# Rounding the weights on GpSimd, one row-sum step per head pair, and early activations rounded on ScalarE: a fused attention and feed-forward kernel on Trainium2

## The chip, the core and the metric

The kernel runs on one core of one Trainium2 chip. A core has five engines with instruction queues of their own: TensorE (PE in the profile; its weight loads are PEld), VectorE (DVE), ScalarE (ACT), GpSimd (POOL) and SyncE (SP), which here issues nearly all DMAs. Each engine runs its queue in order, so an instruction that waits holds everything behind it. The metric is the device time of one execution in microseconds; lower is better. Before the change three timed executions gave 724.78, 723.21 and 723.17 us, median 723.21.

## The reference

```python
# attention: q, k, v of (4, 8, 768, 64) in float32
scores = scale * np.matmul(q, k.transpose(0, 1, 3, 2))
keep = is_sink | in_window            # 4 sink keys, window of 128
scores = np.where(keep, scores, -1000000000.0)
a = np.exp(scores - np.max(scores, axis=-1, keepdims=True))
a = a / (np.sum(a, axis=-1, keepdims=True) + 1e-09)
attn_out = np.matmul(a, v)
# feed-forward on x of (3072, 512), w_in (512, 2048), w_out (2048, 512)
h = x @ w_in
g = h * np.clip(h + 3.0, 0.0, 6.0) / 6.0
out = g @ w_out
```

The two weight matrices arrive as 64-bit floats, which the kernel reads as pairs of 32-bit integers.

## The kernel before

The work is cut into 12 units of 256 tokens (4 batches, 3 token blocks each). A unit has 4 pairs of heads, so there are 48 pairs, numbered s = 0 to 47; the first 16 pairs belong to the first token block of each batch, whose queries see only two key tiles. Pairs 0 to 9 are `plain`: their score, transpose and value products run in full float32 passes. After the 4 pairs of a unit come its feed-forward steps, i = 0 to 7, each on 256 of the 2048 hidden columns: 24 matmuls into `hps` (`ffn1`, line 468), then the activation, then 12 matmuls into the output accumulators `o` (`ffn2`, line 490).

Every product outside the plain pairs is made from rounded pieces. A value x is split into a high part, x rounded to the format `fp32r` that TensorE takes at full rate, and a low part, x minus the high part. `hps` is therefore summed from wih*xh, wih*xl and wil*xh, and `o` from gh*woh, gh*wol and g*woh.

The weights come in 32 pieces of 128x512, in the order wih, wih, woh, woh per step i. `load_part` (line 135) brings a piece into one of four buffers `st` by a DMA on SP, takes its 64-bit words apart on ScalarE (lines 153 and 157) and puts a 32-bit float together on VectorE (lines 159 and 161), in one of three buffers `wt`. Then `copy_r` (line 163) rounds it to the high part, on ScalarE before the change (`WHI = "A"`), and VectorE makes the low part (line 164). A buffer `st` is free for the next DMA when line 161 has read it.

For a plain pair the chain is: scores on TensorE into a PSUM bank (`sp`, line 306); masking and row minimum on VectorE (line 313); exponential and row sum on ScalarE (line 335), one instruction for each of the two query tiles t of each head h; 1e-9 added and the reciprocal taken on VectorE (lines 337, 338); scaling of each block by its reciprocal (`norm`, line 319); transposes on TensorE into `pt` (line 361), copied out by ScalarE as `pf` (line 365); the product with the values, `av` (line 428); and its split into xh and xl for the feed-forward (lines 443, 444). The blocks of t = 0 have 128 columns, those of t = 1 have 256. `NORM0 = "DADA"` gives the engine for the four blocks of pairs 0 to 8: VectorE for the 128-column ones, ScalarE for the 256-column ones; pair 9 and all later pairs scale on ScalarE.

The activation of a feed-forward step is: `gf` on ScalarE (line 476), times the clip on VectorE (line 477), rounded to `gh` (line 478, on VectorE by `GHI = "DD"`), and the low part `g` on VectorE (line 479). `eng` (line 206) takes the letter after the first for the units 0 to 2 (n*NP < START = 9), and the first letter for all later ones.

The loop over s (line 572) interleaves by the string `ORDER`: scores and softmax of pair s-1, values and feed-forward of pair s-2, weight pieces (one per s from 1 to 4, then four per s), and `drain` calls, which emit a feed-forward step only when its weight pieces have been emitted. While pairs 0 to 3 are under way there is no feed-forward work, and `keep_busy` puts dummy matmuls (`idle`) between the scores. The framework then orders the instructions of each engine by its own estimate of when their inputs are ready, so that a change of an engine also changes the order on the others.

Of the kernel before, what the change touches and what calls it, by code (L numbers as in the profile page):

```python
# [14 lines left out]
ALU = mybir.AluOpType  # L15
# [3 lines left out]
P = 128  # L19
# [13 lines left out]
def copy_r(nc, eng, out, src, scale=1.0):  # L33
    if eng is nc.scalar:
        nc.scalar.mul(out=out, in_=src, mul=scale)  # L35
    elif eng is nc.gpsimd:
        nc.gpsimd.tensor_scalar(out=out, in0=src, scalar1=scale, scalar2=1.0, op0=ALU.mult, op1=ALU.mult)
    elif scale != 1.0:
        nc.vector.tensor_scalar(out=out, in0=src, scalar1=scale, scalar2=None, op0=ALU.mult)
    else:  # L40
        nc.vector.tensor_copy(out=out, in_=src)  # L41
# [3 lines left out]
def attn_ffn_kernel(ctx: ExitStack, tc: tile.TileContext, qx, kx, vx, vfx, vsx, n_sink, window, w_in, w_out, out):  # L45
    nc = tc.nc
# [80 lines left out]
    WOH = [const.tile([P, 2, DM], F32R, name=f"woh{i}") for i in range(NFP)]  # L127
    WOL = [const.tile([P, 2, DM], F32R, name=f"wol{i}") for i in range(NFP)]
    wide = mybir.dt.size(w_in.dtype) == 8
    WHI, WLO = "A", "D"  # L130

    def weng(which, at):
        return {"D": nc.vector, "P": nc.gpsimd, "A": nc.scalar}[which[at % len(which)]]
# [65 lines left out]

    SSE = "DD"  # L200
    START = 9
    GHI, GLO = "DD", "DD"
    XHI, XLO = "DDA", "DD"
    KHI, KLO, QHI, QLO = "AA", "DD", "AA", "DD"

# [80 lines left out]
    def cell(s, h, t, c0, c1):  # L286

        if plain(s):
            return st_[s][f"P{h}"][:, t * P + c0:t * P + c1]
        return st_[s]["P"][:, h, t * WP + c0:t * WP + c1]  # L290
# [23 lines left out]
                                       scalar=3.0e38, op0=ALU.add, op1=ALU.min,  # L314
                                       accum_out=d["nb"][:, i:i + 1])

    NORM0, NORM = "DADA", "AAAA"

    def norm(e, blk, c):
        if e == "A":  # L320
            nc.scalar.mul(out=blk, in_=blk, mul=c)  # L321
        elif e == "D":
            nc.vector.tensor_scalar(out=blk, in0=blk, scalar1=c, scalar2=None, op0=ALU.mult)
        else:
            nc.gpsimd.tensor_scalar(out=blk, in0=blk, scalar1=c, scalar2=1.0, op0=ALU.mult, op1=ALU.mult)

    def C_soft(s, h):
# [5 lines left out]
        for t in range(2):  # L333
            i, blk = 2 * h + t, cell(s, h, t, *live[t])
            d["exp"] = nc.scalar.activation(out=blk, in_=blk, func=AF.Exp, scale=-1.0,  # L335
                                            bias=nb[:, i:i + 1], accum_out=sm[:, i:i + 1])
        nc.vector.tensor_scalar(out=sm[:, hs], in0=sm[:, hs], scalar1=1e-9, scalar2=None, op0=ALU.add)
        nc.vector.reciprocal(out=rc[:, hs], in_=sm[:, hs])
        if u:
# [2 lines left out]
            prior = d["P"][:, h, 0:2 * WP].rearrange("p (t w) -> p t w", t=2)[:, :, 0:P]  # L342
            nc.gpsimd.tensor_tensor(out=both, in0=both, in1=prior, op=ALU.add)  # L343
            live = [(P, W2), (P, W2)]
        for t in range(2):
            i, blk = 2 * h + t, cell(s, h, t, *live[t])
            norm((NORM0 if s < START else NORM)[i], blk, rc[:, i:i + 1])
        if u and h == 1:

            ss = ssc.rearrange("p (t k h y) -> p t k h y", t=2, k=2, h=2)  # L350
# [423 lines left out]
```

## Time and profile before

| | |
|---|---|
| median of three timed executions | 723.21 us |
| the profiled execution | 726.12 us |
| its span, first to last instruction | 724.4 us |
| mean granted TensorE clock, share of full speed | 0.996 |
| TensorE busy | 707.9 us, 98% |
| TensorE weight loads busy | 637.9 us, 88% |
| VectorE busy | 494.3 us, 68% |
| ScalarE busy | 424.8 us, 59% |
| GpSimd busy | 169.1 us, 23% |

The shares are means over stages that differ. The last of the weight pieces is finished at some 123 us; until then VectorE and ScalarE do the weights beside the attention of the first pairs and the first feed-forward steps, and GpSimd has nothing to do. From 190.77 us on GpSimd merges and masks blocks of the later pairs. Matmuls overlap in the array, so the duration of one matmul is longer than the distance from one to the next.

### The profile page before, as it was taken

To read this page: it belongs to the slowest core of one execution; us is meant where nothing else is said; L and a number is where in the kernel's file an instruction comes from. 1 tells how busy PE (TensorE), PEld (TensorE's weight loads), DVE (VectorE), ACT (ScalarE), POOL (GpSimd) and SP (SyncE) were. 2 spreads that over 40 slices of the span, in tenths; PEclk is the share of its full clock that TensorE was granted. 3 is DMA by queue.
4 is the path that set the end of the run, shared out by engine and by line. 5 is a ranking of instruction groups with operands and counts; after the bars stand their busy time and mean duration, and the time that the engine had idled before them with its cause. 6 is when DMAs were issued, how large, how long until landed. Compare 5 with 4: busy or idle time off the path is not lost. (4 is left out here: it accounts for less than half of the span.)

```text
span 724.4 us, 14312 instructions
## 1 busy us (share of the span) xinstructions
PE 707.9 (98%) x4772; PEld 637.9 (88%) x4772; DVE 494.3 (68%) x1418; ACT 424.8 (59%) x1139; POOL 169.1 (23%) x336
## 2 busy tenths in 40 slices
PE   8998999999999999999999999999999999999996
PEld 7777787899999999999998999999989999998985
DVE  5798999666775776775866777777676686532231
ACT  6998997656656657566655665655665665311211
POOL 1000000000143243353343343243344253100000
PEclk9999999999999999999999999999999999999999
DMA  7666683544545546445544644644644632000000
GB/s 239 190 190 213 208 249 101 143 108 133 131 124 141 130 120 173 117 113 140 142 108 125 161 119 104 176 109 125 170 107 109 164 81 61 30 1 1 30 1 34
DMA packets 55602, 89.11 MB, mean 123 GB/s; under 512 B 8416, under 2 KB 38368, under 8 KB 55520
## 3 DMA queue, kind: packets, MB, share of 16 engines
q1 hardware_dynamic: 55376, 88.11, 44.7%
q8 instruction: 40, 0.66, 0.4%
q14 instruction: 42, 0.34, 0.2%
q10 hardware_dynamic: 144, 0.00, 0.0%
HBM read 42.47 MB, written 6.29 MB: 67 GB/s over the span
## 5 line engine op out<-in xcount | busy, mean ns | idle before, releaser
L468 PE MATMUL hps<-xh,wih 128*128 128x256 f32 x768 | 221.1, 288 | 4.1 <-ACT wih L35 2.8
L468 PE MATMUL hps<-xh,wil 128*128 128x256 f32 x768 | 217.4, 283 | 0.2 <-DVE wil L164 0.2
L468 PE MATMUL hps<-xl,wih 128*128 128x256 f32 x768 | 216.3, 282 | 0.1
L490 PE MATMUL o<-woh,gh 128*128 128x512 f32 x384 | 154.8, 403 | 2.3 <-DVE gh L41 2.2
L468 PEld LDWEIGHTS hps<-xh,wih 128*128 128x128 f32 x768 | 144.9, 189 | 9.0 <-ACT wih L35 5.6
L490 PE MATMUL o<-wol,gh 128*128 128x512 f32 x384 | 151.3, 394 | 0.0
L490 PE MATMUL o<-woh,g 128*128 128x512 f32 x384 | 151.1, 395 | 0.0
L468 PEld LDWEIGHTS hps<-xl,wih 128*128 128x128 f32 x768 | 145.1, 189 | 0.9 <-DVE xl L444 0.3
L468 PEld LDWEIGHTS hps<-xh,wil 128*128 128x128 f32 x768 | 144.7, 189 | 0.7 <-DVE wil L164 0.4
L335 ACT ACTIVATE Pt<-Pt,nb 128x272 f32<-128x272 f32 (+2 forms) x152 | 76.9, 506 | 77.2 <-DVE nb L313 76.4
L343 POOL TENSOR_TENSOR Pt<-Pt 128x256 f32<-128x256 f32 x64 | 47.4, 740 | 274.8 <-ACT Pt L335 274.8
L477 DVE SCALAR_TENSOR_TENSOR gf<-gf,hps 128x512 f32<-128x512 f32 x96 | 65.8, 685 | 64.2 <-ACT gf L476 61.6
L476 ACT ACTIVATE gf<-hps,three 128x512 f32<-128x512 f32 x96 | 65.5, 683 | 71.5 <-PE hps L468 70.8
L490 PEld LDWEIGHTS o<-woh,g 128*128 128x128 f32 x384 | 72.2, 188 | 16.4
L490 PEld LDWEIGHTS o<-woh,gh 128*128 128x128 f32 x384 | 72.4, 189 | 13.9 <-ACT xh L35 1.6
L321 ACT ACTIVATE Pt<-Pt,rc 128x144 f32<-128x144 f32 (+2 forms) x152 | 55.7, 414 | 44.9 <-POOL Pt L343 39.5
L490 PEld LDWEIGHTS o<-wol,gh 128*128 128x128 f32 x384 | 72.4, 189 | 10.6
L479 DVE TENSOR_TENSOR g<-gf,gh 128x512 fp32r<-128x512 f32 x96 | 69.3, 722 | 1.2 <-PE o L490 0.3
L379 POOL TENSOR_SCALAR_AFFINE_SELECT ph<-ph 128x256 fp32r<-128x256 f32 x64 | 32.4, 510 | 153.0 <-ACT ph L35 153.0
L311 PE MATMUL sp<-K,Q 128*128 128x272 f32 (+2 forms) x304 | 61.5, 286 | 1.5 <-DMA Q<-qt 1.4
L313 DVE CUSTOM_DVE_ANT_0 Pt<-sp,m_t 128x272 f32<-128x272 f32 x128 | 54.0, 432 | 11.1 <-PE sp L311 10.2
L311 PEld LDWEIGHTS sp<-K,Q 128*128 128x128 f32 x304 | 51.4, 188 | 8.9 <-DVE xl L452 0.8
(96 smaller groups left out, 1080.6 us busy)
## 6 DMA issues: line engine op xcount, KB each, us to landing
K<-kt SPq DMA_DIRECT2D x128, 200.0 KB, 3.5
Q<-qt SPq DMA_DIRECT2D x152, 64.0 KB, 2.5
st<-in_w_in_dram SPq DMA_DIRECT2D x16, 512.0 KB, 4.1
st<-in_w_out_dram SPq DMA_DIRECT2D x16, 512.0 KB, 5.1
kr<-in_kx_dram SPq DMA_DIRECT2D x32, 200.0 KB, 2.5
qr<-in_qx_dram SPq DMA_DIRECT2D x48, 128.0 KB, 2.2
out_dram<-ost SPq DMA_DIRECT2D x24, 256.0 KB, 2.4
vr<-in_vx_dram SPq DMA_DIRECT2D x32, 192.0 KB, 2.5
```

The lines of the kernel that those rows point to most:

```text
L311: nc.tensor.matmul(out=sp[:, 0:w], lhsT=Q[:, h, t * P:(t + 1) * P], rhs=K[:, h, part, k0c:k0c + w], start=(part == 0), stop=(part == 1))
L313: d["min"] = nc.vector.tensor_tensor_reduce(out=cell(s, h, t, 0, w), in0=sp[:, 0:w], in1=m[:, 0:w], scale=-SCALE, scalar=3.0e38, op0=ALU.a ...
L321: nc.scalar.mul(out=blk, in_=blk, mul=c)
L335: d["exp"] = nc.scalar.activation(out=blk, in_=blk, func=AF.Exp, scale=-1.0, bias=nb[:, i:i + 1], accum_out=sm[:, i:i + 1])
L343: nc.gpsimd.tensor_tensor(out=both, in0=both, in1=prior, op=ALU.add)
L379: nc.gpsimd.affine_select(out=prior[i], in_=own[i], pattern=[[0, 2], [-1, P]], base=0, channel_multiplier=1, compare_op=ALU.is_gt, fill=0.0)
L468: nc.tensor.matmul(out=hp[:, half, :], lhsT=l, rhs=r, start=(j == 0), stop=(j == n - 1))
L476: nc.scalar.activation(out=gf, in_=hp, func=AF.Relu, bias=three, scale=1.0)
L477: nc.vector.scalar_tensor_tensor(out=gf, in0=gf, scalar=6.0, in1=hp, op0=ALU.min, op1=ALU.mult)
L479: eng(GLO, state["n"] * NP).tensor_tensor(out=g, in0=gf, in1=gh.bitcast(F32), op=ALU.subtract)
L490: nc.tensor.matmul(out=acc, lhsT=l[:, f, ts_], rhs=r[i][:, f, :], start=(i == 0 and f == 0 and j == 0), stop=(i == NFP - 1 and f == 1 and ...
```

## The change

Five edits. `copy_r` on GpSimd becomes a `tensor_copy` instead of a two-operand scaling (no call used GpSimd before). `WHI` goes from ScalarE to GpSimd: all 32 weight pieces get their high part there. `NORM0` goes from `DADA` to `PAPA`: the 128-column blocks of pairs 0 to 8 are scaled by GpSimd (line 325). In a plain pair the softmax end runs once per pair: after the exponentials of head 0 `C_soft` returns, and after those of head 1 the additions and reciprocals of all four sums are one instruction each on 128x4, followed by the four scalings. `GHI` goes from `DD` to `DA`: `gh` of units 0 to 2 is rounded on ScalarE.

```diff
     elif eng is nc.gpsimd:
-        nc.gpsimd.tensor_scalar(out=out, in0=src, scalar1=scale, scalar2=1.0, op0=ALU.mult, op1=ALU.mult)
+        nc.gpsimd.tensor_copy(out=out, in_=src)
...
-    WHI, WLO = "A", "D"
+    WHI, WLO = "P", "D"
...
-    GHI, GLO = "DD", "DD"
+    GHI, GLO = "DA", "DD"
...
-    NORM0, NORM = "DADA", "AAAA"
+    NORM0, NORM = "PAPA", "AAAA"
...
+        heads = [h]
+        if plain(s):
+            if h == 0:
+                return
+            heads, hs = [0, 1], slice(0, 4)
...
-        for t in range(2):
-            i, blk = 2 * h + t, cell(s, h, t, *live[t])
-            norm((NORM0 if s < START else NORM)[i], blk, rc[:, i:i + 1])
+        for g in heads:
+            for t in range(2):
+                i, blk = 2 * g + t, cell(s, g, t, *live[t])
+                norm((NORM0 if s < START else NORM)[i], blk, rc[:, i:i + 1])
```

In the changed file the lines behind the edits stand five or six lower: 337 and 338 are 342 and 343, 361 is 367, 428 is 434, 476 is 482. On VectorE, at the end of the softmax of pair 0 (`sm` holds the row sums, `rc` their reciprocals, `Ph` one head's blocks, `st` a weight piece), the difference reads:

```order
-L337 TENSOR_SCALAR sm<-sm 128x2
-L338 RECIPROCAL rc<-sm 128x2
-L323 TENSOR_SCALAR Ph<-Ph,rc 128x128
-L337 TENSOR_SCALAR sm<-sm 128x2
-L338 RECIPROCAL rc<-sm 128x2
-L323 TENSOR_SCALAR Ph<-Ph,rc 128x128
+L342 TENSOR_SCALAR sm<-sm 128x4
+L343 RECIPROCAL rc<-sm 128x4
 L159 SCALAR_TENSOR_TENSOR st<-st 128x512
```

Six instructions of VectorE become two, behind the exponentials of both heads. On TensorE, from the transposes of pair 1 to the scores of pair 2 (`pt` the transposes, `av` the value products of pair 0, `sp` the scores of pair 2), the difference reads:

```order
-L361 MATMUL pt<-ident_r,Ph 128x128 x4
+L434 MATMUL av<-pf,VF 128x256
+L434 MATMUL av<-pf,VF 128x128
+L434 MATMUL av<-pf,VF 128x256
+L434 MATMUL av<-pf,VF 128x128
+L367 MATMUL pt<-ident_r,Ph 128x128 x6
 L306 MATMUL sp<-kr,qr 128x128
 L306 MATMUL sp<-kr,qr 128x256
-L361 MATMUL pt<-ident_r,Ph 128x128 x2
 L81 MATMUL idle<-rel 128x128 x4
```

The scores of pair 2 stood between the transposes of pair 1, ahead of the last two; now they stand behind all six. On GpSimd, from the last of the mask copies on, there stood before:

```order
L187 COPY m_t_99<-m_t_98 128x128
L116 TENSOR_SCALAR m_t_98<-col 128x16
L189 COPY m_t_99<-m_t_98 128x128
L188 COPY m_t_99<-m_t_98 128x16
L343 TENSOR_TENSOR Pt<-Pt 128x2x128 x2
```

where the last row belongs to a pair of the second token block (190.77 us). Now, in the same place (`wih_111` and `woh_127` are the high parts of step 0, `wih_112` of step 1):

```order
L188 COPY m_t_99<-m_t_98 128x16
L325 TENSOR_SCALAR Ph<-Ph,rc 128x128 x2
L37 CAST wih_111<-wt 128x512 x2
L325 TENSOR_SCALAR Ph<-Ph,rc 128x128 x2
L37 CAST woh_127<-wt 128x512
L325 TENSOR_SCALAR Ph<-Ph,rc 128x128 x2
L37 CAST woh_127<-wt 128x512
L37 CAST wih_112<-wt 128x512
L325 TENSOR_SCALAR Ph<-Ph,rc 128x128 x2
L37 CAST wih_112<-wt 128x512
```

A stretch of 32 casts and 18 scalings now stands ahead of the row of line 343 (348 in the changed file); both casts of step 0's wih stand ahead of the scalings of pair 1. The third place is the first activation of a feed-forward step (`hps` its matmuls' sum, `wol` the low part of a weight piece). On VectorE there stood before:

```order
L477 SCALAR_TENSOR_TENSOR gf<-gf,hps 128x512
L313 ISA Ph,nb<-sp,m_100 128x128
L313 ISA nb 128x1
L41 CAST gh<-gf 128x512
L164 TENSOR_TENSOR wol_136<-wt,woh_128 128x512
L479 TENSOR_TENSOR g<-gf,gh 128x512
```

The rounding `gh` is on ScalarE in the changed order, whose rows there read:

```order
L482 ACTIVATE gf<-hps,three 128x512
L35 ACTIVATE pf<-pt 128x384
L157 ACTIVATE st<-st 128x512
L153 ACTIVATE wt<-st 128x512
L35 ACTIVATE gh<-gf 128x512
```

Between `gf` and `gh` the queue of ScalarE holds a copy and two weight instructions of other work, and VectorE's part of `gf` lies in between; before, `gh` followed on the same engine.

## Rows read from the trace of the kernel before

**Rows 1.** Busy time by stretch (window in us, its length, then busy us and number of instructions of PE, PEld, DVE, ACT and POOL, mean granted TensorE clock, DMA share, GB/s): the first pairs, the first feed-forward steps, the rest of the weight stage, and 100 us from the middle.

```profile
0.00:34.00 34.00, 31.71 (x197) 25.97 (x198) 23.21 (x97) 25.91 (x74) 3.09 (x16) 1.00 0.67 216
34.00:80.00 46.00, 40.68 (x231) 32.48 (x229) 41.01 (x106) 40.60 (x95) 0.00 (x0) 0.96 0.63 195
80.00:132.40 52.40, 51.27 (x325) 44.05 (x324) 48.76 (x130) 46.54 (x116) 0.00 (x0) 1.00 0.62 183
...
300.00:400.00 100.00, 100.00 (x694) 91.56 (x693) 70.30 (x209) 61.11 (x173) 38.51 (x72) 1.00 0.52 130
```

**Rows 2.** What TensorE waited for from 0 to 133 us (instruction, what released it: us in total, times, longest).

```profile
PE hps L468 <- ACT wih L35: 2.8, 3, 2.2
PE o L490 <- DVE gh L41: 2.2, 2, 1.4
...
PE hps L468 <- DVE gf L477: 0.9, 1, 0.9
...
PE pt L361 <- ACT Ph L321: 0.3, 1, 0.3
```

**Rows 3.** TensorE alone around its longest wait (window, length, busy us, granted clock, DMA share, GB/s).

```profile
61.70:63.90 2.20, 0.01 (x1) 0.94 0.08 18
63.90:67.10 3.20, 3.18 (x13) 0.51 0.51 166
```

**Rows 4.** Instructions in order of time (start, duration, engine, line, what; in brackets the idle time before and what ended it) that lead to this wait: SP's queue, ScalarE and VectorE.

```profile
54.36 0.93 SPq L148 DMA_DIRECT2D st<-in_w_out_dram  x2
...
59.52 0.66 ACT L153 ACTIVATE wt<-st 128x512 f32<-128x512 f32 x1 [1.27 <-DMA st<-in_w_out_dram]
...
63.24 0.62 ACT L35 ACTIVATE wih<-wt 128x512 fp32r<-128x512 f32 x1
...
60.71 0.17 DVE L337 TENSOR_SCALAR sm<-sm 128x2 f32<-128x2 f32 x1 [1.37 <-ACT Ph L335]
...
61.90 0.68 DVE L161 SCALAR_TENSOR_TENSOR wt<-wt,st 128x512 int32<-128x512 int32 x1
```

**Rows 5.** Groups of instructions from 0 to 132.4 us (line, engine, operation, tiles, shapes, count, busy us, mean ns of one, idle before and releaser), on VectorE and, the last, on ScalarE.

```profile
L159 DVE SCALAR_TENSOR_TENSOR st<-st 128x512 int32<-128x512 int32 x32 | 21.9, 686 | 1.7 <-ACT st L157 1.7
L161 DVE SCALAR_TENSOR_TENSOR wt<-wt,st 128x512 int32<-128x512 int32 x32 | 21.4, 685 | 0.1
L164 DVE TENSOR_TENSOR wil<-wt,wih 128x512 fp32r<-128x512 f32 x16 | 10.9, 687 | 1.0 <-ACT wih L35 0.9
L164 DVE TENSOR_TENSOR wol<-wt,woh 128x512 fp32r<-128x512 f32 x16 | 10.9, 686 | 1.0 <-ACT woh L35 0.9
...
L323 DVE TENSOR_SCALAR Ph<-Ph,rc 128x128 f32<-128x128 f32 x18 | 5.1, 283 | 0.3
L41 DVE CAST gh<-gf 128x512 fp32r<-128x512 f32 x11 | 4.6, 421 | 0.2 <-PE o L490 0.2
...
L35 ACT ACTIVATE wih<-wt 128x512 fp32r<-128x512 f32 x16 | 10.0, 622 | 0.0
```

**Rows 6.** Pairs of rows in order of time from which the distance of one start to the next is read, where the engine had no pause: a weight rounding on ScalarE; the rounding `gh` on VectorE; and row sum, reciprocal and scaling of one head on VectorE, with the next instruction behind them.

```profile
38.85 0.63 ACT L35 ACTIVATE wih<-wt 128x512 fp32r<-128x512 f32 x1
39.36 0.69 ACT L476 ACTIVATE gf<-hps,three 128x512 f32<-128x512 f32 x1
...
42.73 0.42 DVE L41 CAST gh<-gf 128x512 fp32r<-128x512 f32 x1
43.07 0.68 DVE L164 TENSOR_TENSOR wol<-wt,woh 128x512 fp32r<-128x512 f32 x1
...
17.56 0.16 DVE L337 TENSOR_SCALAR sm<-sm 128x2 f32<-128x2 f32 x1
...
18.16 0.42 DVE L444 TENSOR_TENSOR xl<-av,xh 128x256 fp32r<-128x256 f32 x1
```

**Rows 7.** Pair 1 in order of time: TensorE's transposes, the scores of pair 2 and the last transposes; and on ScalarE the last exponential and the last scaling of pair 1.

```profile
18.30 0.33 PE L361 MATMUL pt<-ident_r,Ph 128*128 128x128 f32 x1 [0.58 <-DVE Ph L323]
18.56 0.92 PE L306 MATMUL sp<-kr,qr 64*128 64x128 f32 x4
19.41 0.44 PE L361 MATMUL pt<-ident_r,Ph 128*128 128x128 f32 x2
...
16.50 0.49 ACT L335 ACTIVATE Ph<-Ph,nb 128x256 f32<-128x256 f32 x1
...
18.35 0.50 ACT L321 ACTIVATE Ph<-Ph,rc 128x256 f32<-128x256 f32 x1
```

**Rows 8.** Groups on GpSimd over the whole span (columns as in rows 5): its only cast to `fp32r`, and its scaling instructions of 128 columns.

```profile
L116 POOL TENSOR_SCALAR m_t<-rel 128x128 bf16<-128x128 f32 x2 | 0.6, 298 | 4.5 <-DVE rel L112 4.5
...
L72 POOL CAST ident_r<-ident 128x128 fp32r<-128x128 f32 x1 | 0.3, 293 | 0.1
```

**Rows 9.** GpSimd and VectorE beside each other at 309 to 313 us, in order of time, and the group of VectorE's `qt` from 40 to 122 us, while GpSimd had no work.

```profile
309.59 0.40 POOL L379 TENSOR_SCALAR_AFFINE_SELECT pl<-pl 128x256 fp32r<-128x256 f32 x1
...
312.02 0.89 POOL L381 TENSOR_SCALAR_AFFINE_SELECT pl<-pl 128x256 fp32r<-128x256 f32 x1
...
309.62 0.65 DVE L30 TENSOR_TENSOR qt<-qr,qt 128x256 fp32r<-128x256 f32 x1
...
311.96 0.69 DVE L479 TENSOR_TENSOR g<-gf,gh 128x512 fp32r<-128x512 f32 x1
...
L30 DVE TENSOR_TENSOR qt<-qr,qt 128x256 fp32r<-128x256 f32 x2 | 0.8, 420 | 0.0
```

## The prediction

> **What bounds the kernel now.** I read the page's first two sections first, then the busy times by stretch, then what TensorE waited for, then the order of time around the waits. TensorE is busy 98% of the span, so nothing that only makes another engine shorter is worth anything, unless TensorE waits for it. The reader should look for the difference between the length of a stretch and TensorE's busy time in it [rows 1]: 34.00 - 31.71 = 2.3 us in the first stretch, 46.00 - 40.68 = 5.3 in the second, 52.40 - 51.27 = 1.1 in the third, and nothing from 300 to 400 us. The order of TensorE's instructions before and after the change is the same from the instruction that runs at 132.4 us on, and the instructions ahead of it are the same ones in another order, so the change can move only what TensorE loses in the first 132.4 us. There VectorE (41.0 of 46 us, then 48.8 of 52.4) and ScalarE (40.6, then 46.5) are as full as an engine in a queue of waits gets [rows 1], and they feed TensorE's weights and activations.
>
> The waits name it [rows 2]: 2.8 us for a rounded weight piece `wih`, 2.2 for `gh`, 0.9 for a buffer that `gf` frees, 0.3 and (the row at 18.30 [rows 7]) 0.58 for scaled blocks. The longest, 2.20 us at 61.7, also costs clock: in the 3.20 us behind it the granted clock was 0.51, the 1.2 GHz level [rows 3], so 3.18 us of matmuls took about 1.6 us longer than at full clock. What the change could win at most is therefore 0.9 (scaled blocks) + 5.3 + 1.1 + 1.6 = 8.9 us, 8.0 of them from 34 us on.
>
> **The change part by part.** The sum is made against the profiled execution, 726.12 us with a span of 724.4; the median of the runs shown is 723.21, 2.9 lower, and I subtract the same amount from it.
>
> Weights on GpSimd. ScalarE loses 32 roundings at one start per 0.51 us (38.85 to 39.36 [rows 6]), 16.3 us. GpSimd gets 32 casts of 512 columns. The trace has no such cast; the nearest rows are a cast of 128 columns at 0.293 us [rows 8] and a one-input select of 256 at 0.40 [rows 9]. That is 0.107 for 128 columns more, so 512 columns take about 0.40 + 2 x 0.107 = 0.61 us as an estimate; the same select beside VectorE took 0.89, which would make the cast 0.61 + 0.49 = 1.10. I take 0.61 to 1.10, and 0.8 as the middle, because VectorE is at work nearly all the time there. 32 x 0.8 = 26 us on an engine that is idle in this stage [rows 1]: this by itself costs nothing. On the path of a piece it replaces a wait in ScalarE's queue. At the long stall line 161 ended at 61.90 + 0.68 = 62.58, ScalarE began the rounding at 63.24 and ended at 63.86 [rows 4]; GpSimd would end it at about 63.4.
>
> Scalings on GpSimd and one softmax end per pair. For each head VectorE spent 0.60 us on sum, reciprocal and scaling (17.56 to 18.16 [rows 6]); 18 such heads in pairs 0 to 8 are 10.8 us, of which nine pairs keep two instructions of 0.2, so 7.2 us go, and 0.4 for pair 9: 7.6. GpSimd gets 18 scalings at 0.30 [rows 8], 5.4 us.
>
> `gh` on ScalarE. VectorE loses 0.34 us (42.73 to 43.07 [rows 6]) for each of 11 roundings up to 132.4 us [rows 5], 3.7 us; the other 13 come later, where ScalarE is 61% busy [rows 1] and has room. ScalarE gets 11 x 0.51 = 5.6 us. So in the weight stage ScalarE is relieved of 16.3 - 5.6 = 10.7 us and VectorE of 7.6 + 3.7 = 11.3.
>
> What GpSimd takes back from VectorE. Where both work at once, one is held up: VectorE's `qt` took 0.65 beside GpSimd and 0.42 without it, while `g` took 0.69, its usual time, and GpSimd's select under it 0.89 instead of 0.40 [rows 9]. So a GpSimd instruction costs VectorE between nothing and 0.23 us, when it meets an instruction with two operands in SBUF; these are 21.9 + 21.4 + 10.9 + 10.9 = 65 us [rows 5] of the 112 from 10 to 122 us, 58%. 50 new GpSimd instructions x 0.58 x (0 to 0.23) = 0 to 6.7 us. I take 3.5, as both rows occur side by side. VectorE's relief is then 11.3 - 3.5 = 7.8 us. The Trainium skill bears on this (GPSIMD Engine Reference, 1. Specifications): GpSimd's interfaces to SBUF are shared with VectorE, which contends when it runs in a 2-port mode or with two inputs from SBUF. Rows 9 agree, in both directions; the rule says nothing about who is held up, and if it were always VectorE, the sum would be that of the fourth case below.
>
> What TensorE gets from it. First the pairs, to 34 us. The scores of pair 2 stood ahead of the last two transposes of pair 1, now they stand behind all six. Before, the transposes and scores ended at 19.41 + 0.44 = 19.85 [rows 7]. Now nothing of pair 1's transposes need run before both heads' scalings are there, and ScalarE's last one ended at 18.35 + 0.50 = 18.85; six transposes and the scores (0.33 x 2 + 0.44 + 0.92, about 1.8 us with overlaps) would end at 20.6, 0.8 later. But the rounding of 0.51 no longer stands ahead of this scaling in ScalarE's queue, which leaves about 0.3. The bounds for pairs 1 to 3 are -0.9 (the two waits of rows 2 and 7 vanish) and 3 x 1.3 = 3.9 (the whole 1.3 from 18.56 to 19.85 is added each time); I take 3 x 0.3 = +0.8 or so.
>
> Then 34 to 80 us. The chain of the long stall runs: a DMA issued at 54.36 that kept ScalarE waiting 1.27 us, an exponential late by that, VectorE held 1.37 us in front of its row sum, line 161 late, ScalarE's queue, `wih` [rows 4]. Every link behind the DMA is an instruction that the change takes from the queue or shortens: one row sum per pair instead of two halves the places where VectorE can be caught like this, and a free `st` buffer comes earlier when line 161 does, and with it the DMA. I expect the waits for `wih` (2.8) and the clock loss (1.6) to go but for some 0.5, and of the 2.2 for `gh` half to stay, because `gh` now stands behind up to three ScalarE instructions (about 0.5 each) though TensorE's new order puts it a step later: the 12 `o` matmuls of a step mostly follow the `hps` of the next one. So 5.3 + 1.6 = 6.9 become 1.5, a gain of 5.4. What is late next is then VectorE itself, at the low parts of the weights. From 80 to 132.4 us TensorE lost 1.1 and I add 0.4 for `gh`. Sum: +0.8 - 5.4 + 0.4 = -4.2. Span 724.4 - 4.2 = 720.2, that execution 721.9, median 723.21 - 4.2 = 719.0.
>
> **The rivals.** Second case, all waits go: VectorE and ScalarE each have 8 to 11 us less in a stage where TensorE misses 8.9; then 723.21 - 8.9 = 714.3. For it: the relief is as large as the loss. Against it: queues this full still collide, and the early pairs hardly gain.
>
> Third case, the DMA sets the pace: the four `st` buffers and SP's queue, in which the weights stand behind the loads of the pairs, stay as they are, and the 1.27 us for the DMA [rows 4] recur. Only the ScalarE queue time is won, 0.5 us at each of the three `wih` waits [rows 2], 1.5 us, and the pairs take 0.8 back, `gh` the rest: 723, no change. For it: ScalarE waited for a DMA just ahead of the stall. Against: that DMA itself waited for line 161.
>
> Fourth case, slower: VectorE pays for the port. The place is the weight stage, the price is what a GpSimd instruction costs VectorE where they meet, and it decides above 11.3 / 50 = 0.23 us per instruction. If VectorE were held for a whole cast of 0.61 and scaling of 0.30 at 58%, that is (32 x 0.61 + 18 x 0.30) x 0.58 = 14.5 us, 3.2 more than the relief; TensorE would then wait those 3.2 longer, as VectorE feeds it, with 1.6 for one more drop of the clock, and 0.8 in the pairs: 723.21 + 5.6, about 728.8. For it: `qt` at 0.65. Against: `g` at 0.69 beside a GpSimd at 0.89 [rows 9]. That the rounding does not move to GpSimd can't be: its order shows 32 casts.
>
> **How the numbers follow.** Forecast 0.45, with a range of its own from 716.5 to 721; all waits go 0.17; no change 0.20; slower 0.18. The range 714.5 to 725.5 leaves out the lowest end of the second case and the upper half of the fourth, about 2 in 10. A measurement of this kernel tells 0.3%, 2.2 us, from no change: faster 0.45 + 0.17 = 0.62, same 0.20, slower 0.18.
>
> **What would show it.** In the new profile TensorE's idle time from 34 to 80 us should be near 1.5 instead of 5.3, with no stretch at the lower clock; GpSimd's casts at 0.6 to 1.1 us; VectorE's lines 159, 161 and 164 at 0.69 to 0.85 on average; the first `hps` matmul at 34 to 35 us. The forecast is wrong if TensorE still stops for 2 us before a `wih` or `wil`, if a new pause opens before the transposes of pairs 1 to 3 (over 1 us each, the clock falling behind it), or if VectorE's weight instructions average above 0.9 us.

## The result and the profile after

The change made the kernel slower. Four executions of the changed kernel gave 731.30, 736.26, 737.38 and 739.33 us, median 736.82; the kernel before, run beside it, had 724.0 (723.17 to 726.76). The ratio is 1.0137, 95% interval [1.0094, 1.0179]. A later set of runs gave 1.0095 [1.0065, 1.0125] (below). The profiled execution is the fastest of the four, with a span of 729.3 us against 724.4, so its profile shows only a part of the loss.

Busy time by stretch after the change (columns as in [rows 1]):

```profile
0.00:34.00 34.00, 27.60 (x176) 23.10 (x177) 20.47 (x73) 22.91 (x63) 10.93 (x29) 1.00 0.66 219
34.00:80.00 46.00, 38.93 (x232) 30.33 (x232) 37.25 (x91) 35.83 (x88) 17.53 (x21) 1.00 0.59 192
80.00:132.40 52.40, 49.90 (x316) 42.33 (x314) 46.04 (x111) 40.92 (x99) 14.38 (x17) 1.00 0.59 178
```

Take TensorE's busy time from the length, as in the prediction: it now loses 6.4, 7.1 and 2.5 us, where it lost 2.3, 5.3 and 1.1 [rows 1]. That is 7.3 us more. Against it stands the clock, which was 0.96 from 34 to 80 us before (46 x 0.04 = 1.8 us) and is 1.00 here. The difference, 5.5, is about that of the spans, 4.9. VectorE and ScalarE have less to do in each stretch and yet feed TensorE worse. What TensorE waited for over the whole span, after (compare [rows 2]):

```profile
PE pt L367 <- POOL Ph L325: 9.9, 10, 2.1
PE o L496 <- ACT gh L35: 2.1, 1, 2.1
...
PE hps L474 <- POOL wih L37: 1.1, 3, 0.5
```

The wait for `wih` fell from 2.8 to 1.1 us with none over 0.5; the forecast left some 0.5 of it and of the clock loss together. The new one is in the first row: ten waits of the transposes for the blocks that GpSimd scales. The groups on GpSimd, over the whole span (columns as in [rows 5]):

```profile
L325 POOL TENSOR_SCALAR Ph<-Ph,rc 128x128 f32<-128x128 f32 x18 | 15.2, 858 | 7.4 <-ACT wt L153 6.8 <-DVE rc L343 0.6
L37 POOL CAST wih<-wt 128x512 fp32r<-128x512 f32 x16 | 12.7, 796 | 44.6 <-DVE wt L161 44.6
L37 POOL CAST woh<-wt 128x512 fp32r<-128x512 f32 x16 | 12.2, 765 | 24.3 <-DVE wt L161 24.3
```

A cast takes 0.78 us on average, and a scaling of a quarter of the size 0.86. The instructions in order of time say why. First GpSimd (start, duration; x2 is the two scalings of one pair together), at pairs 0 and 1:

```profile
10.98 0.72 POOL L325 TENSOR_SCALAR Ph<-Ph,rc 128x128 f32<-128x128 f32 x2 [2.33 <-ACT wt L153]
...
17.55 0.61 POOL L37 CAST wih<-wt 128x512 fp32r<-128x512 f32 x1 [2.96 <-DVE wt L161]
18.14 1.67 POOL L325 TENSOR_SCALAR Ph<-Ph,rc 128x128 f32<-128x128 f32 x2
```

Then VectorE at pair 1, and TensorE's transposes of pairs 1 and 3:

```profile
16.80 0.68 DVE L161 SCALAR_TENSOR_TENSOR wt<-wt,st 128x512 int32<-128x512 int32 x1
17.40 0.17 DVE L343 RECIPROCAL rc<-sm 128x4 f32<-128x4 f32 x1
17.85 0.85 DVE L159 SCALAR_TENSOR_TENSOR st<-st 128x512 int32<-128x512 int32 x1 [0.28 <-ACT st L157]
18.63 0.68 DVE L164 TENSOR_TENSOR wil<-wt,wih 128x512 fp32r<-128x512 f32 x1
```

```profile
19.52 0.89 PE L367 MATMUL pt<-ident_r,Ph 128*128 128x128 f32 x6 [2.02 <-POOL Ph L325]
...
33.52 0.90 PE L367 MATMUL pt<-ident_r,Ph 128*128 128x128 f32 x4 [2.08 <-POOL Ph L325]
```

Two delays stand in these rows. **The queue:** line 161 ends at 17.48 and releases a cast; the reciprocal stands directly behind it and ends at 17.57. The cast is already running, so the scalings, whose operands are ready at 17.57, begin at 18.14, 0.57 late. A scaling is late behind a cast at five of the nine pairs (0.57, 1.03, 0.56, 0.57 and 0.37 us), at the first four of these with the reciprocal directly behind line 161 as here. **The hold:** the two scalings took 0.72 us at pair 0, but 1.67 beside VectorE's lines 159 and 164. From the reciprocal's end to the last scaled block of pair 1, that is 2.24 us, and TensorE stopped for 2.02. The longest hold of one scaling is at pair 4, where TensorE had feed-forward matmuls to do and did not stop. GpSimd first, then VectorE in the same time:

```profile
38.90 0.61 POOL L37 CAST woh<-wt 128x512 fp32r<-128x512 f32 x1 [2.46 <-DVE wt L161]
39.49 1.44 POOL L325 TENSOR_SCALAR Ph<-Ph,rc 128x128 f32<-128x128 f32 x1
40.91 0.80 POOL L325 TENSOR_SCALAR Ph<-Ph,rc 128x128 f32<-128x128 f32 x1
```

```profile
39.48 0.69 DVE L159 SCALAR_TENSOR_TENSOR st<-st 128x512 int32<-128x512 int32 x1 [0.25 <-ACT st L157]
40.09 0.68 DVE L164 TENSOR_TENSOR wol<-wt,woh 128x512 fp32r<-128x512 f32 x1
40.70 0.78 DVE L161 SCALAR_TENSOR_TENSOR wt<-wt,st 128x512 int32<-128x512 int32 x1
```

The first scaling begins 0.01 us behind line 159 and ends at 40.93, behind two whole instructions of VectorE (39.48 to 40.77), which stand back to back; the second ends behind line 161. An instruction of 0.36 us so took 1.44. VectorE itself paid little: its weight groups from 0 to 132.4 us, next to [rows 5], rose from 685 to 687 ns to

```profile
L159 DVE SCALAR_TENSOR_TENSOR st<-st 128x512 int32<-128x512 int32 x32 | 22.2, 702 | 2.1 <-ACT st L157 2.1
L161 DVE SCALAR_TENSOR_TENSOR wt<-wt,st 128x512 int32<-128x512 int32 x32 | 22.1, 696 | 0.0
L164 DVE TENSOR_TENSOR wil<-wt,wih 128x512 fp32r<-128x512 f32 x16 | 11.4, 710 | 2.1 <-POOL wih L37 1.9
L164 DVE TENSOR_TENSOR wol<-wt,woh 128x512 fp32r<-128x512 f32 x16 | 11.3, 709 | 3.4 <-POOL woh L37 3.4
```

### The profile page after: what moved, and what is told of

Same layout as the page of the kernel before. It is cut to its first block, busy times and chain, and to the rows that moved or that the text cites. A ratio compares the mean times of both kernels' runs of the same rounds, so it can differ in the third digit from the quotient of the medians.

```text
span 729.3 us, 14327 instructions
## 1 busy us (share of the span) xinstructions
PE 705.5 (97%) x4772; PEld 635.4 (87%) x4772; DVE 484.4 (66%) x1356; ACT 423.6 (58%) x1131; POOL 209.3 (29%) x386
## 4 chain that ended last, share of the span: by engine, by line
PE 83%; DVE 5%; DMA 4%; POOL 2%; issue 2%; ACT 2%; SPq 1%; DVEq 0%; POOLq 0%; ACTq 0%
PE hps L474 34%; PE o L496 33%; PE av L434 6%; PE sp L311 5%; PE pt L367 3%; PE sp L306 2%; POOL Ph L325 1%; DMA Q<-qt 1%; DVE wt L161 1%; DMA st<-in_w_out_dram 1%; PE idle L81 1%; DMA raw<-in_n_sink_dram 1%; DMA K<-kt 1%; SPq L261 1%; DVE Ph L313 1%
```

## The experiments

The theory: the scalings on GpSimd lie on TensorE's path and are late there because they share a queue with the casts and are held beside VectorE. The rivals: the casts alone cost it (`wih` comes late), the single softmax end per pair costs it (the blocks of both heads come at once and late), or the early relief is real and the clock alone makes the loss. All ratios are to the kernel before, run on the same chip. In the table "pair" means one softmax end per pair and "head" one per head; the 128-column scalings are those of pairs 0 to 8.

| weights rounded on | 128-column scalings on | softmax end | `gh` of units 0 to 2 | median us | ratio, 95% interval |
|---|---|---|---|---|---|
| GpSimd | GpSimd | pair | ScalarE | 731.83 | 1.0095 [1.0065, 1.0125] |
| GpSimd | VectorE | pair | ScalarE | 724.48 | 0.998 [0.9955, 1.0005] |
| GpSimd | ScalarE | pair | ScalarE | 723.61 | 0.9969 [0.995, 0.9988] |
| the same again | | | | 723.76 | 0.9974 [0.9953, 0.9994] |
| GpSimd | one of two on GpSimd | pair | ScalarE | 725.83 | 1.0034 [1.0016, 1.0051] |
| ScalarE | GpSimd | pair | ScalarE | 726.22 | 1.0008 [0.9986, 1.003] |
| ScalarE, and read by GpSimd | GpSimd | pair | ScalarE | 734.27 | 1.013 [1.0084, 1.0177] |
| GpSimd | GpSimd | head | ScalarE | 729.20 | 1.0052 [1.0034, 1.007] |
| GpSimd | VectorE | head | ScalarE | 726.02 | 1.0002 [0.9983, 1.0021] |
| GpSimd | ScalarE | head | ScalarE | 726.01 | 1.0011 [0.9996, 1.0025] |
| GpSimd | VectorE | head | VectorE | 727.82 | 1.0026 [1.0, 1.0051] |
| ScalarE | GpSimd | head | VectorE | 725.77 | 0.9999 [0.9973, 1.0025] |
| ScalarE | VectorE | pair | VectorE | 726.83 | 1.0006 [0.9977, 1.0034] |

**One part of the change undone.** The changed kernel with the scalings back on VectorE, and with the casts back on ScalarE:

```diff
-    NORM0, NORM = "PAPA", "AAAA"
+    NORM0, NORM = "DADA", "AAAA"
```

> The changed kernel with only the 128-column scalings of pairs 0 to 8 put back on VectorE; one softmax end per pair, casts on GpSimd and gh on ScalarE stay. Theory A (the scalings on GpSimd make the loss: 9.9 us of TensorE's waits in the changed kernel end with them, each beside VectorE instructions with two SBUF operands): TensorE's wait for a scaled block falls below 2 us, the span to 718 to 722 us, faster than before by 0.3 to 0.8%. Theory B (the single softmax end per pair makes the loss, whoever scales): the waits before the transposes stay at 6 us or more, and the time stays at 729 us or above. Theory C (the casts on GpSimd or gh on ScalarE make it): also no better than 728.

```diff
-    WHI, WLO = "P", "D"
+    WHI, WLO = "A", "D"
```

> The changed kernel with only the weight roundings put back on ScalarE, so that the 18 scalings are alone on GpSimd. If the scalings are slow because casts stand ahead of them in GpSimd's queue: the scaling's mean stays near 0.86 us only where VectorE collides, but TensorE's wait for it falls from 9.9 to under 4 us. If VectorE's two-operand instructions hold them up: their mean stays above 0.7 us, with TensorE waiting 6 us or more, and the time is 730 or above.

Either of them takes the loss away: 0.998 and 1.0008. The gain of 0.3 to 0.8% that the first was expected to show is not clear of noise. With the casts back on ScalarE the scalings still wait and are still held, but less: 0.605 us each, and TensorE's waits for them are 2.9 us in all, the longest 0.8. With the scalings on VectorE, the busy times by stretch and the first wait are:

```profile
0.00:34.00 34.00, 29.37 (x188) 24.30 (x188) 23.53 (x84) 24.36 (x67) 6.61 (x21) 1.00 0.66 219
34.00:80.00 46.00, 43.81 (x260) 34.02 (x258) 42.41 (x109) 38.50 (x94) 12.35 (x15) 1.00 0.68 216
80.00:132.40 52.40, 50.41 (x323) 43.89 (x323) 46.50 (x112) 41.41 (x105) 10.17 (x12) 1.00 0.62 184
```

```profile
PE pt L367 <- DVE Ph L323: 3.0, 3, 1.6
```

From 34 to 80 us TensorE loses 2.2 instead of 5.3 us at a clock of 1.00. That, with the clock, is nearly the gain that was forecast there; the first stretch gives 2.3 of it back (4.6 against 2.3 lost), the third 0.9.

**One part done alone.** The kernel before with the casts alone on GpSimd, with the scalings alone there, and with the single softmax end alone (its diff is that of `C_soft` in the change):

```diff
-        nc.gpsimd.tensor_scalar(out=out, in0=src, scalar1=scale, scalar2=1.0, op0=ALU.mult, op1=ALU.mult)
+        nc.gpsimd.tensor_copy(out=out, in_=src)
...
-    WHI, WLO = "A", "D"
+    WHI, WLO = "P", "D"
```

> The kernel before with only the weight roundings moved to GpSimd (as tensor_copy). Theory A: harmless or a gain, as nothing that TensorE waits for soon is held by a cast of 0.6 to 1.1 us: 718 to 724 us. Theory C: slower by 0.5% or more, with TensorE waiting over 4 us for wih or wil.

```diff
-    NORM0, NORM = "DADA", "AAAA"
+    NORM0, NORM = "PAPA", "AAAA"
```

> The kernel before with only the 128-column scalings of pairs 0 to 8 moved to GpSimd, each head ending by itself. Theory A: slower by 0.5 to 1.5% (728 to 735 us), TensorE waiting over 4 us for scaled blocks, scalings at 0.7 to 0.9 us on average. Theory B: within 0.4% of before.

```diff
+        heads = [h]
+        if plain(s):
+            if h == 0:
+                return
+            heads, hs = [0, 1], slice(0, 4)
```

> The kernel before with only the single softmax end per pair (scalings on VectorE and ScalarE, casts on ScalarE). If the serial chain behind both heads costs by itself: 0.8 us or more per pair for pairs 1 to 3, slower by 0.4% or more (727 or above). If it costs only together with late scalings: within 0.3% of before.

The ratios are 1.0026, 0.9999 and 1.0006; none alone makes 1.0095. The scalings alone took 0.600 us each, and TensorE's longest wait for one was 0.8, so that they are enough by themselves (728 to 735 us) is refuted. The loss is thus an interaction: it needs casts and scalings together in GpSimd's queue. No run has the whole change with `gh` alone put back. `gh` on ScalarE stands in both versions above that lose nothing, so it is not enough by itself; whether it adds to the loss beside the other parts is not shown. The changed kernel run once more beside these gave a smaller loss than the first time, and it shows how much of it varies:

> The changed kernel once more, unchanged, beside the others on one chip. In the first four runs its time rose as its clock fell: 731.3 us at 0.997, 739.3 at 0.982. Both theories of the clock expect 731 to 739 us and ratios of 1.009 to 1.018 again; if those four runs were an accident of that chip, below 1.006.

Its five executions were 730.52 and 730.70 us at a mean clock of 0.998, 731.83 at 0.995, and 735.45 and 735.74 at 0.989 and 0.991. Its profiled one has a span of 733.7 us, 4.4 more than the first profile of the same kernel. Windows of that first profile (span 729.3), then of this one:

```profile
17.00:20.00 3.00, 0.98 (x8) 0.72 (x7) 2.36 (x5) 1.88 (x5) 2.26 (x3) 1.00 0.62 189
20.00:23.00 3.00, 3.00 (x20) 2.17 (x18) 1.43 (x6) 1.97 (x6) 0.60 (x1) 1.00 0.45 158
```

```profile
17.00:20.00 3.00, 0.97 (x8) 0.72 (x7) 2.37 (x5) 1.90 (x5) 2.27 (x3) 1.00 0.67 215
20.00:23.00 3.00, 3.00 (x13) 2.17 (x13) 1.24 (x5) 1.84 (x6) 0.00 (x0) 0.55 0.35 135
23.00:26.00 3.00, 3.00 (x11) 2.12 (x11) 0.76 (x6) 0.62 (x4) 0.61 (x1) 0.50 0.48 156
26.00:29.00 3.00, 3.00 (x13) 2.82 (x13) 1.02 (x5) 2.02 (x5) 0.72 (x2) 0.50 0.36 109
```

The same stop of 2.0 us for the same scaled blocks stands in both. Behind it the granted clock stayed at 1.00 in the one and was 0.50 (1.2 GHz) for some 10 us in the other. A kernel with such a stop has a time with two parts: the stop itself, and a fall of the clock that follows in some executions and not in others. The kernel before has such executions too: of the 13 beside this set, eight at a mean clock of 0.998 or more took 724.39 to 726.10 us, and four at 0.990 to 0.992 took 728.83 to 729.63.

**Dummy matmuls ahead of the stops.** Six more `idle` matmuls behind the scores of head 1 of pairs 1 to 3, in the changed kernel, and in the versions with the scalings on VectorE and on ScalarE:

```diff
-                    keep_busy(WARM[2])
+                    keep_busy(WARM[2] + 6 * h)
```

> The changed kernel with 6 more dummy matmuls (about 1.45 us) behind the second head's scores of pairs 1 to 3, where TensorE waited 2.0 us in pairs 1 and 3. If the executions of 736 to 739 us are slower than that of 731 because the clock falls behind these waits: the granted clock is 0.995 or more in all runs, and the median falls by 2 to 6 us to 731 to 734, though TensorE has 4.4 us more to do. If the lower clock has another place or cause: median 737 or above, clock 0.98 to 0.99 as before.

> The changed kernel with the scalings back on VectorE and six more idle matmuls per odd slot of the first pairs. If what is left there is a clock that falls behind short pauses in some executions, the spread shrinks and the time is 722.5 to 724.5, level with or just below the kernel before. If the clock plays no part, the added matmuls (about 0.07 us each at full clock) only cost, and it is 724.5 to 727.

> The version with all early scalings on ScalarE, with six more idle matmuls per odd slot of the first pairs. If the clock that falls in the first stretch in some executions costs it time, 721.5 to 723.3 with less spread. If not, the added matmuls cost about 0.5 us and more: 723.6 to 725.

In the changed kernel they gain: 729.44 us, ratio 1.0051 [1.0032, 1.0069], with all four executions at a clock of 0.998 or 0.999. The six take 1.34 us of TensorE each time, far more than the 0.07 each of the second expectation, and fill a part of the stops: at pair 1 TensorE then waits 0.95 us for scaled blocks in place of 2.02. In the others they don't gain: 725.09 us, 0.999 [0.9972, 1.0008], and 723.96, 0.9987 [0.997, 1.0003]. So a part of the loss is the fall of the clock, and a part stays when the clock is steady: with the added matmuls the executions took 727.95 to 729.90 us, without them those at 0.998 took 730.52 and 730.70, some 2 to 5 us more than the 725.54 of the kernel before beside them. That the clock alone makes the loss is refuted.

**The softmax end per head again.** In the changed kernel, then with the scalings on VectorE and on ScalarE (the diff is the reverse of that in `C_soft`):

> The changed kernel without the single softmax end per pair: each head ends by itself, as before; casts and scalings on GpSimd and gh on ScalarE stay. Alone, neither casts nor scalings on GpSimd cost over 0.3%. Theory D (casts and scalings together on GpSimd are enough: a scaling waits behind a cast, and both beside VectorE): scalings at 0.75 us or more, TensorE waits 6 us or more for scaled blocks, 729 us or above. Theory E (the single end is needed too: only with it do all six transposes of a pair hang on the last scaling): wait for scaled blocks under 4 us, within 0.4% of before.

> The kernel before with the casts on GpSimd and the second rounding of gh on ScalarE, and nothing else: softmax ends per head, scalings where they were. If the relief of VectorE and ScalarE is worth what the prediction said and only GpSimd's scalings spoil it, 719 to 722. If the relief is worth little because the next wait in the weight stage takes its place, 723.5 to 727.

> All early scalings on ScalarE, casts on GpSimd, the second gh rounding on ScalarE, but the softmax ends once per head as in the kernel before. If the single end per pair is a loss by itself that the version with all scalings on ScalarE still pays, 721 to 723. If it is a relief for VectorE there (two small instructions fewer per pair), 724 to 726.

The ratio goes from 1.0095 to 1.0052 with the scalings on GpSimd, from 0.998 to 1.0002 with them on VectorE, and from 0.9969 to 1.0011 on ScalarE. Casts and scalings together on GpSimd thus lose with the ends apart too (theory D, though the 0.73 us of a scaling and the 5.5 us of waits fall just short of its figures). The single end seems to add to the loss there, but the two intervals just overlap; on ScalarE it is a gain of about 0.4% (the intervals don't overlap), on VectorE no difference can be told. As a cause by itself it falls. With the ends apart, a single scaling behind a single cast ended a stop of 2.55 us at pair 3, of which 1.49 lie between the end of the reciprocal (32.29) and that of the scaling (33.78):

```profile
33.83 0.48 PE L361 MATMUL pt<-ident_r,Ph 128*128 128x128 f32 x1 [2.55 <-POOL Ph L325]
```

The version with the scalings on VectorE and the ends apart is also the relief of VectorE and ScalarE by itself. At 726.02 us it is not the 719 to 722 that the prediction would give. From 34 to 80 us it loses only 1.9 us, but the first stretch loses 4.0, 1.76 of them at pair 3. There GpSimd's cast took 1.01 us, VectorE stood before its low part (line 164) for it, ahead of the row sum, and TensorE stopped for a block that VectorE scales:

```profile
29.38 1.01 POOL L37 CAST woh<-wt 128x512 fp32r<-128x512 f32 x1 [6.97 <-DVE wt L161]
...
30.43 0.69 DVE L164 TENSOR_TENSOR wol<-wt,woh 128x512 fp32r<-128x512 f32 x1 [0.51 <-POOL woh L37]
...
32.53 0.74 PE L361 MATMUL pt<-ident_r,Ph 128*128 128x128 f32 x3 [1.76 <-DVE Ph L323]
```

**All early scalings on ScalarE, twice.**

```diff
-    NORM0, NORM = "PAPA", "AAAA"
+    NORM0, NORM = "AAAA", "AAAA"
```

> The changed kernel with the two scalings of a pair that GpSimd got on ScalarE instead. If the scalings on GpSimd beside its casts are the loss, TensorE waits for no scaled block over 1.2 us and the time is 723 to 726, as with these scalings on VectorE. If the single softmax end for both heads is what opens the pauses, they stay at 2 us and the time is 728 to 732.

> The version with all early scalings on ScalarE once more, on another chip run. If its 0.3% over the kernel before is real, the ratio is again 0.995 to 0.999 and the median 722.5 to 724 against some 725; if it was chance, the interval holds 1.

Both sets agree (0.9969 and 0.9974, neither interval holding 1): this version beats both kernels, by 0.3% the kernel before. TensorE's longest waits for scaled blocks were 0.9 us. The first run's stretches (the clock of 0.95 is a fall in that execution; the second run's profile has 1.00 there):

```profile
0.00:34.00 34.00, 30.73 (x179) 24.98 (x180) 20.86 (x73) 24.49 (x70) 6.18 (x21) 0.95 0.67 212
34.00:80.00 46.00, 44.93 (x266) 35.34 (x266) 41.41 (x102) 41.46 (x104) 13.34 (x15) 1.00 0.69 215
80.00:132.40 52.40, 50.27 (x316) 42.89 (x316) 47.22 (x110) 42.81 (x108) 11.18 (x13) 1.00 0.63 183
```

From 34 to 80 us 1.1 us are lost, less than the 1.5 that were forecast.

**Half of the scalings on GpSimd.**

```diff
-    NORM0, NORM = "PAPA", "AAAA"
+    NORM0, NORM = "DAPA", "AAAA"
```

> The changed kernel with one of the two scalings on VectorE again, so 9 on GpSimd instead of 18. If the loss is the time that the scalings are queued and held on GpSimd, it is about halved with half of them: waits for scaled blocks at 3 to 6 us in all, none over 1.4, and 726 to 729. If the loss comes as soon as any scaling stands behind a cast in GpSimd's queue (the wait is for the last block of a pair, however many there are), TensorE still stops for 2 us and the time is 730 to 734.

1.0034, about a third of the loss for half of the scalings; the median, 725.83, lies just below the 726 to 729 expected. TensorE waited 0.8 us for GpSimd's blocks (longest 0.4) and 2.3 for VectorE's, though at pairs 1 and 3 a scaling again stood behind a cast. That one scaling behind a cast always opens a stop of 2 us is refuted; that two in a row are needed is refuted by the 2.55 us above.

**Casts that nobody waits for.** The version with the casts on ScalarE and the scalings on GpSimd, in which GpSimd besides copies 384 columns of every weight piece into a scratch tile:

```diff
         copy_r(nc, weng(WHI, at), hi, like(ft))
+        nc.gpsimd.tensor_copy(out=junk, in_=ft[:, 0:384])
```

> The real roundings on ScalarE, scalings on GpSimd, and GpSimd besides reads 384 columns of every weight piece into a scratch tile that nobody uses. If the loss is GpSimd's queue (scalings behind a cast that waits for VectorE's weight instruction, and held beside it), waits for scaled blocks rise from 2.9 us in all (longest 0.8) to 6 to 10 (longest 1.5 to 2.1), scalings from 0.60 us to 0.75 or more, and the ratio is 1.005 to 1.013 though no result of GpSimd's casts is ever waited for. If the loss came from taking the casts off ScalarE (another order on the engines) or from wih being late, it stays at 1.001 and waits at 2.9.

The ratio goes from 1.0008 to 1.013. What TensorE waited for, and the two groups on GpSimd:

```profile
PE pt L370 <- POOL Ph L328: 7.3, 8, 1.7
```

```profile
L166 POOL CAST junk<-wt 128x384 bf16<-128x384 f32 x32 | 23.1, 721 | 76.3 <-DVE wt L163 57.6 <-DVE rc L346 14.0 <-DVE sm L345 4.6
L328 POOL TENSOR_SCALAR Ph<-Ph,rc 128x128 f32<-128x128 f32 x18 | 11.8, 667 | 12.5 <-ACT wt L155 9.0 <-DVE rc L346 3.5
```

The waits for scaled blocks rise from 2.9 to 7.3 us though no later instruction uses these copies. That the result of a cast comes late is excluded with that, and so is the lighter ScalarE. The scalings themselves rose only to 0.667 us, below the 0.75 expected. What this run can't separate is a second price of the copies: each also keeps one of the three `wt` buffers until GpSimd has read it, so the weights can be late by GpSimd's queue as well; TensorE's waits for weight pieces rose from 0.7 to 1.7 us.

**The hold by itself.** A kernel that does nothing but six casts and twelve scalings on GpSimd, in seven stretches, beside VectorE with one kind of instruction:

> Leaves out the whole computation: it only repeats GpSimd's scaling of 128 columns and its cast of 512 while VectorE does one kind of instruction at a time. If GpSimd is the one held wherever VectorE reads two operands from SBUF, scalings go from 0.36 us alone to 0.8 to 1.2 and casts from 0.61 to 0.8 to 1.1 beside VectorE's subtraction and its shift of 512 columns from SBUF, and stay at 0.36 and 0.61 beside the instructions that read PSUM; VectorE's own stay at 0.69. If the long scalings of the changed kernel come from something else (the wait for a semaphore, data that come late), all stretches show 0.36 and 0.61. If both engines pay, VectorE's instructions are above 0.8 as well.

The framework mixed the kinds in this first try, and most of the casts and scalings ran beside copies out of PSUM (casts 0.61 to 0.65 us there), so it doesn't settle the question. The second one ties them by their data (`pool_work` is GpSimd's part):

```diff
+    pool_work(3)
+    for _ in range(N):
+        nc.vector.tensor_copy(out=o0, in_=a0)
...
+    pool_work(5)
+    for _ in range(N):
+        nc.vector.tensor_tensor(out=r0, in0=a0, in1=b0, op=ALU.subtract)
```

> Leaves out the whole computation: in seven stretches GpSimd does six casts of 512 columns and twelve scalings of 128 while VectorE does nothing, or 30 (60 in one stretch) instructions of one kind in fixed order. If GpSimd is held wherever VectorE reads two operands from SBUF, scalings go from 0.36 us to 0.8 to 1.2 and casts from 0.61 to 0.8 to 1.1 in the last two stretches (subtraction and shift of 512 columns from SBUF) and stay at 0.36 and 0.61 beside the instructions that read one operand or PSUM. If one operand in SBUF is enough, the stretches with VectorE's copy and its own scaling show it too. If the long scalings of the changed kernel come from something else, all stretches show 0.36 and 0.61. If both engines pay, VectorE's own durations rise too while GpSimd works.

GpSimd in order of time (x2 and x4 together): with VectorE idle, beside a subtraction of a PSUM from an SBUF operand, beside a copy with one SBUF operand, and beside a subtraction of two SBUF operands:

```profile
8.32 1.28 POOL L74 CAST wih<-wt 128x512 fp32r<-128x512 f32 x2
9.70 1.76 POOL L76 TENSOR_SCALAR wih<-wih,rc 128x128 f32<-128x128 f32 x4
...
40.89 1.29 POOL L74 CAST wih<-wt 128x512 fp32r<-128x512 f32 x2
42.27 1.76 POOL L76 TENSOR_SCALAR wih<-wih,rc 128x128 f32<-128x128 f32 x4
...
63.58 1.43 POOL L74 CAST wih<-wt 128x512 fp32r<-128x512 f32 x2
65.10 1.95 POOL L76 TENSOR_SCALAR wih<-wih,rc 128x128 f32<-128x128 f32 x4
...
105.11 1.96 POOL L74 CAST wih<-wt 128x512 fp32r<-128x512 f32 x2
107.17 3.01 POOL L76 TENSOR_SCALAR wih<-wih,rc 128x128 f32<-128x128 f32 x4
```

and VectorE's groups, beside two SBUF operands (first row) and beside one from PSUM:

```profile
L95 DVE TENSOR_TENSOR r<-a,b 128x512 fp32r<-128x512 f32 x30 | 23.1, 770 | 1.3 <-POOL wih L71 0.3
...
L86 DVE TENSOR_TENSOR r<-a,pp 128x512 fp32r<-128x512 f32 x30 | 20.6, 688 | 1.3 <-POOL wih L71 0.3
```

A scaling goes from 0.44 to 0.75 us and a cast from 0.64 to 0.98 beside two SBUF operands, little beside a copy with one (0.49 and 0.72), and not at all beside one from SBUF and one from PSUM. VectorE pays too: (770 - 691) x 30 = 2.4 us, where 691 ns is the shortest of the group, over some 18 GpSimd instructions, 0.13 us each. Beside its one-operand instructions VectorE pays as much or more:

```profile
L92 DVE TENSOR_SCALAR r<-r,rc 128x128 f32<-128x128 f32 x60 | 20.6, 344 | 2.4 <-POOL wih L71 0.3
L89 DVE COPY r<-a 128x512 f32<-128x512 f32 x30 | 15.1, 504 | 1.3 <-POOL wih L71 0.3
```

The shortest of these groups are 285 and 426 ns, so VectorE lost (344 - 285) x 60 = 3.5 us on its scalings and (504 - 426) x 30 = 2.3 on its copies. Which engine is held thus depends on VectorE's instruction; that GpSimd is held beside two SBUF operands is shown. Its size is smaller here: the two engines take turns, one scaling for each VectorE instruction (a scaling begins every 0.78 us), while at 39.49 in the changed kernel VectorE went first twice in a row. Why turns are taken here and were not taken there stays open.

## Why the prediction was wrong

It forecast 719.0 us, faster; 736.82 came, outside the range.

- **The step that failed** is the one line on the scalings: "GpSimd gets 18 scalings at 0.30, 5.4 us", put beside the casts on an engine with nothing to do. The price was read from a stretch where VectorE did little; in the weight stage they took 0.86 us, 15.2 in all. Worse, they were priced as work off the path. They are the last link before TensorE's transposes, and the queue that they joined had just been given 32 casts. The prediction's own order of GpSimd showed both casts of step 0's `wih` ahead of the scalings of pair 1 and still no wait was priced there.
- **The port** was weighed with the wrong payer. VectorE's part was inside its bounds of 0 to 6.7 us: taken at 3.5, while the four weight groups rose by (16 + 11) x 32 + (23 + 23) x 16 ns = 1.6 us, and beside two SBUF operands it pays 0.13 us per GpSimd instruction, between 0 and 0.23. But GpSimd paid (0.86 - 0.36) x 18 = 9 us on the scalings alone, and the prediction gave that no place, since GpSimd was idle on average. The slower case had the right resource and the wrong end of it: it wanted VectorE's instructions slow, and TensorE stopped with VectorE at 0.70 us. The Trainium skill (GPSIMD Engine Reference, 1. Specifications) says that the interface is contended when VectorE has two inputs from SBUF; the stretches with one kind at a time agree, 0.75 us against 0.44. Another page of the Trainium skill (SBUF — State Buffer, SBUF: two separate sides) says that of the two the instruction that starts first has the port to its end while the other stands still. By that rule a scaling would be an estimated 0.36 + 0.69 = 1.05 us at worst. The 0.80 us at 40.91 lie within it; the 1.44 before it go beyond it.
- **The first pairs**, +0.8 us, measured +4.1. The single end explains only a part at most: with the scalings back on VectorE the stretch loses 2.3 us more than before, but with the ends apart as well it still loses 1.7 more, and with the casts alone moved 1.6. What these three share is the casts on GpSimd, and in the rows above VectorE's queue waits for one ahead of pair 3's row sum, for which the prediction had no term; whether that is the whole reason is not shown. The upper bound named was 3.9; the value near the lower end was the wrong choice.
- **From 34 to 80 us**, -5.4, measured 7.1 - 5.3 - 1.8 = 0. The mechanism was right where the scalings are not on GpSimd: 1.1 and 2.2 us lost instead of 5.3, no clock loss, `wih` waits short. The casts cost what was estimated, 0.61 alone and up to 1.08 beside VectorE. The `gh` wait of 2.1 us stayed, longer than forecast.
- **The relief** was sized too large even where GpSimd scales nothing. The forecast was -4.2 us, 0.6%; with the scalings on VectorE or ScalarE and the casts and `gh` moved, the ratios are 0.9969 to 1.0011, at best 0.3%. The gain from 34 to 80 us came in most of them, but those versions lose 3.0 to 4.6 us in the first stretch (2.3 before) and 2.0 to 2.8 in the third (1.1 before, 1.5 forecast).
- **The clock** was taken as a loss that would go, and its 1.6 us were taken off the median as well as off the profiled execution. It was lost again elsewhere, behind the new stops, and in some executions only. An execution of the kernel before near 723 us seems to have little of this to give back: of the 31 beside the first experiments, the sixteen at a clock of 0.998 or more took 723.66 to 725.58 us, and the eight at 0.994 or less 727.91 to 730.65.
- The signs named for a wrong forecast included a new pause before the transposes of pairs 1 to 3 of over 1 us with the clock behind it. That is what came, at pairs 1 and 3, with the clock behind it in some executions; it had no price of its own in the sum and no rival.

## What to carry to other kernels

An idle engine is free only for work that nobody waits for: before a step on the critical path is moved there, list what else the same change puts into that engine's queue, and which event releases each. Here a VectorE instruction released a cast just before the scalings became ready, and at five of the nine pairs the cast went first. Price an instruction on GpSimd from a stretch in which VectorE does what it will do beside it, and test two moves to one engine separately and together, since neither alone showed the loss.

## What was not expected of the hardware

- GpSimd is held by VectorE's instructions with two SBUF operands more than it holds them, and can be passed over twice in a row: +0.31 us on a scaling of 0.44 and +0.34 on a cast of 0.64, against +0.13 us on VectorE per GpSimd instruction. Beside a VectorE copy or scaling with one SBUF operand it is mostly VectorE that pays.
- The same stop of 2.0 us at the same place left the clock at 1.00 in one execution and at 0.50 for some 10 us in another; executions of one kernel so differ by 4 to 8 us.
